# Centred rows for V and z2 of the first two blocks, their transposes by DMA, and z2's weights loaded from two queues

## The chip, the cores and the metric

The kernel runs on one core of a Trainium2 chip. The metric is the device time of one execution in microseconds (us). A core has five engines that run beside each other: TensorE (PE, matmuls into PSUM), VectorE (DVE), ScalarE (ACT), GpSimd (POOL) and SyncE (SP). SP mostly issues DMAs; ACT and POOL can issue DMAs too. Each engine executes its own instructions in order, and engines wait for each other by semaphores.

## What is computed

For x of 2048 rows and 512 columns, xn is x normalised by row. The output is x, plus a sliding attention (32 heads of 16, 8 positions 2 apart), plus a gated MLP whose gate mixes all rows:

```python
xn = _layernorm(x, axis=-1)                      # (x - m) / sqrt(v + eps)
# branch A: q, k, v = xn @ wqkv; each row attends to rows s, s-2, ..., s-14; then @ wo
# branch B:
z = _gelu(einsum('bsd,df->bsf', xn, w_in))       # 2 x 896 columns
z1 = z[..., :896]
z2 = _layernorm(z[..., 896:], axis=-1)
g = einsum('ts,bsf->btf', w_sp, z2) + b_sp[None, :, None]
branch_B = einsum('bsf,fd->bsd', z1 * g, w_out)
return x + A + branch_B
```

All tensors are bf16; sums are in f32.

## The kernel before

The rows are cut in 16 blocks of 128. `build_kernel` makes a list of tasks (matmul groups, activations, DMAs) with what they read and write, and `Plan.schedule` simulates them with estimated durations to find one fixed order for each engine and the PSUM banks. `Plan.emit` then writes each engine's instructions in that order, with the waits that the data needs. So each engine's order is fixed before the run: where a real landing is later than the planner thinks, the engine stands. The planner's inputs include priorities (`prio`), lists of names that must follow each other on an engine (line 1003 on), and a table `land` with assumed landing times of the first loads.

What happens to a block b at the start:

- `ld_x(b)` (L514) loads 128 rows of x. x0 and x1 go out from ACT's queue, the others from SP's.
- `ln_block(b)` (L592 on) computes the row statistics on DVE, `bnst` (L599), `bnag` (L601) and `vpe` (L609, variance plus eps), then 1/sqrt on POOL (`rstd`, L611), then the normalised rows on DVE (`norm`, L623).
- For blocks 0 to 3 (`b < NXT`) PE transposes the normalised rows by four matmuls with the identity (`xTr`, L579), and ACT copies them from PSUM to `xnT` (`xTe`, L587). For blocks 4 to 15 a DMA transposes them, issued by SP (`xTd`, L617).
- `v_block(b)` (L654) makes V of the block by four matmuls; ACT evicts it (`Ve`, L663), POOL writes it to a scratch in DRAM (`Vw`, L668).
- `z2_block(b)` (L766) makes 896 columns of z2 in two halves of 448, four matmuls each. The halves of the weights are two loads, w_in2a (L524) and w_in2b (L530). ACT applies the gelu (L774) and sums squares (L779).

V of blocks 0 and 1 does not wait for the normalised rows. PE transposes raw x (`xTx`, L579), ACT copies it to `xcT` (`xTc`, L606), V is made of raw rows, and the mean is taken out afterwards: four matmuls of ones with V's weights give the weights' column sums (`cs`, L638), ACT stores them negated (`cse`, L642), DVE adds mean times column sum to V in PSUM (`fix`, L660), and `Ve` scales with rstd. z2 of blocks 0 and 1 waits for the normalised and transposed rows.

Then `qk_pair` (L677) makes Q and K of four blocks at a time (it reads `xnT` of all four and the weights wq and wk, `ldq` and `ldk`, L536). DVE multiplies Q and shifted K (L698, L703); PE sums over the head dimension (`red`, L713); the softmax follows. PE makes z1 (L812) and then, for most of the time, the mixing of the rows (`g_group`, L907); the output blocks (L963, L972) end the kernel.

SP's DMAs at the start are wv (two halves, L518), x2, w_in2a, w_in2b, x3 to x7, wq, wk, x8 to x15; then the transposes of blocks 4 to 7, w_in1 (L853), and the transposes of blocks 8 to 15. Before x0 lands PE multiplies ones (`warm`, L560).

Of the kernel before, what the change touches and what calls it, by code (L numbers as in the profile page):

```python
# [9 lines left out]
F32 = mybir.dt.float32  # L10
# [328 lines left out]
def build_kernel(nc, A_x, A_wqkv, A_wo, B_x, B_w_in, B_w_sp, B_b_sp, B_w_out, out, report=False, emit=True):  # L339
# [12 lines left out]
    NWARM = 8  # L352
# [18 lines left out]
    place(3584, w_in1=0, tg=0, On=2048, xcT=0, ncs=1024)  # L371
# [14 lines left out]
    for name, n in (("prime", 4), ("mx", 128), ("Zb", 256), ("Z", 128), ("maskt", 128), ("st6", NB * 6),  # L386
                    ("mv", NB * 2), ("vpe", NB), ("rstd", NB), ("s1", NB), ("s2", NB), ("m2", NB), ("msq", NB),
                    ("vpe2", NB), ("rstd2", NB), ("mhalf", 4)):
        foff[name] = fb
        fb += n  # L390
# [5 lines left out]
    with ExitStack() as es:  # L396
# [69 lines left out]
        for hf in range(2):  # L466
            for b in range(2):
                R1(("xcT", b, hf), "xcT", 256, 512 * b + 256 * hf)
            R(("xnT", 0, hf), "sb", [(off["xnT"] + dc * S, off["xnT"] + dc * S + 128) for dc in (2 * hf, 2 * hf + 1)])
        R1("ncs", "ncs", 1024)  # L470
        R1("bbc", "bbc", S)
        R1("w_in1", "w_in1", 3584)
        R("w_in2a", "sb", [(off["w_in2"] + dc * 896, off["w_in2"] + dc * 896 + 448) for dc in range(4)])
# [27 lines left out]
        ncs = A("ncs", 1024).bitcast(F32)  # L501
# [21 lines left out]
        def ld_win2a():  # L523
            dma("sp", lambda e: e.dma_start(  # L524
                AC(off["w_in2"], [[896, 4], [1, 448]]),
                B_w_in[:, 896:1344].rearrange("(c p) n -> p c n", p=128)),
                512 * 448 * 2, "w_in2a", writes=["w_in2a"], name="ldwin2a")
# [45 lines left out]
        def pe_tr(src, keys, name):  # L573
            bk = plan.bank(name)

            def tr(t):
                last = None
                for dc in range(4):
# [3 lines left out]
            T("pe", tr, reads=keys + ["ident"], writes=[bk], est=(430.0 if name == "xTx0" else 4 * c_mm(128)), name=name)  # L582
            return bk

        def to_xnT(b, bk, halves, prio=0, after=()):
            for d0, dn in (((0, 2), (2, 2)) if halves else ((0, 4),)):
                T("act", (lambda d0, dn: lambda a: a.activation(  # L587
                    AC(off["xnT"] + d0 * S + 128 * b, [[S, dn], [1, 128]]),
                    P(bk, 128 * dn, 128 * d0).rearrange("p (c n) -> p c n", c=dn), ACTF.Copy))(d0, dn),
                  reads=[bk], writes=([("xnT", b, d0 // 2)] if halves else [("xnT", b)]), est=c_act(128 * dn),  # L590
                  name="xTe%d_%d" % (b, d0), prio=prio)

        def ln_block(b):
# [4 lines left out]

            T("dve", lambda v: v.bn_stats(Fv("st6", 6, 6 * b), xin), reads=xk, writes=[("st6", b)],  # L599
# [3 lines left out]
            if b < 2:  # L603
                bc = pe_tr(xin, xk, "xTx%d" % b)
                for hf in range(2):
                    T("act", (lambda hf: lambda a: a.activation(A("xcT", 256, 512 * b + 256 * hf), P(bc, 256, 256 * hf),  # L606
                                                                ACTF.Copy))(hf),
                      reads=[bc], writes=[("xcT", b, hf)], est=c_act(256), name="xTc%d_%d" % (b, hf), prio=-1)
            T("dve", lambda v: v.tensor_scalar(Fv("vpe", 1, b), Fv("mv", 1, 2 * b + 1), LN_EPS, None, ALU.add),  # L609
              reads=[("mv", b)], writes=[("vpe", b)], est=140, name="vpe%d" % b, prio=-1.5 + b * 0.1)  # L610
# [3 lines left out]
            if b < NXT:  # L614
                to_xnT(b, pe_tr(xn, [("xn", sl)], "xTr%d" % b), b == 0)
# [13 lines left out]
        def xTv(b, dc):  # L629
            return AC(off["xnT"] + dc * S + 128 * b, [[1, 128]])  # L630

        def colsum():
            bk = plan.bank("cs")
            for hf in range(2):
                def mm(t, hf=hf):
                    last = None
                    for dc in (2 * hf, 2 * hf + 1):
                        last = t.matmul(P(bk, 512), ones[:, 0:128], A("wv", 512, 512 * dc), start=(dc == 0),  # L638
                                        stop=(dc == 3))
                    return last  # L640
                T("pe", mm, reads=[("wv", hf)], writes=[bk], est=2 * c_mm(512) * (1 if hf else 2), name="cs_%d" % hf, prio=2)
            T("act", lambda a: a.activation(ncs, P(bk, 512), ACTF.Copy, scale=-1.0), reads=[bk],  # L642
              writes=["ncs"], est=c_act(512), name="cse", prio=-0.5)

        def v_block(b):
# [4 lines left out]
            for hf in range(2):  # L650
                def mm(t, hf=hf):
                    last = None
                    for dc in (2 * hf, 2 * hf + 1):
                        last = t.matmul(P(bk, 512), A("xcT", 128, 512 * b + 128 * dc) if b < 2 else xTv(b, dc),  # L654
                                        A("wv", 512, 512 * dc), start=(dc == 0), stop=(dc == 3))
                    return last
                T("pe", mm, reads=[("xcT", b, hf) if b < 2 else ("xnT", b), ("wv", hf)], writes=[bk],
                  est=2 * c_mm(512) * (1.5 if (b, hf) == (0, 0) else 1), name="V%d_%d" % (b, hf), prio=(2 if b < 4 else 60 + b))
            if b < 2:
# [3 lines left out]
            T("act", lambda a: a.activation(vn.rearrange("p (d h) -> p d h", d=16),  # L663
                                            PC(bk.col(), [[1, 16], [16, 32]]), ACTF.Copy,
                                            scale=Fv("rstd", 1, b) if b < 2 else 1.0),
              reads=[bk] + ([("rstd", b)] if b < 2 else []), writes=[("Vn", sl)], est=c_act(512), name="Ve%d" % b,
              prio=4)
# [91 lines left out]
        def z2_block(b):  # L759
            bk = plan.bank("z2_%d" % b, 2)  # L760
            for hf in range(2):
                for dcs in (((0, 1), (2, 3)) if b == 0 and hf == 0 else ((0, 1, 2, 3),)):
                    def mm(t, hf=hf, dcs=dcs):
                        last = None
                        for dc in dcs:
                            last = t.matmul(P(bk, 448, 512 * hf), xTv(b, dc),  # L766
                                            AC(off["w_in2"] + 896 * dc + 448 * hf, [[1, 448]]),
                                            start=(dc == 0), stop=(dc == 3))
                        return last
                    T("pe", mm, reads=([("xnT", 0, dcs[0] // 2)] if len(dcs) == 2 else [("xnT", 0, 0), ("xnT", 0, 1)] if b == 0 else [("xnT", b)]) +  # L770
                      ["w_in2b" if hf else "w_in2a"],
                      writes=[bk], est=len(dcs) * c_mm(448),
                      name="z2_%d_%d" % (b, hf) + ("b" if dcs == (2, 3) else ""), prio=12 + 4 * b)
            T("act", lambda a: a.activation(A("z2", FH, FH * b).rearrange("p (t n) -> p t n", t=2),  # L774
                                            PC(bk.col(), [[512, 2], [1, 448]]),
                                            ACTF.Gelu_apprx_tanh, accum_out=Fv("s1", 1, b)),
              reads=[bk], writes=[("z2", b), ("s1", b)], est=c_act(FH, accum=True),
# [49 lines left out]
        colsum()  # L827
        v_block(0)
        v_block(1)
        lnd += [ln_block(b) for b in range(2, NB)]  # L830
# [172 lines left out]
        for names in (["warm%d" % wi for wi in range(NWARM)] +  # L1003
                      ["xTx0", "cs_0", "V0_0", "xTx1", "cs_1", "V0_1", "xTr0", "V1_0", "xTr1", "V1_1",
                       "z2_0_0", "z2_0_0b", "z2_0_1", "xTr2", "z2_1_0", "z2_1_1", "V2_0", "V2_1", "xTr3", "z2_2_0"],
                      ("rstd4", "Vw0"),
                      ("bnst0", "bnag0", "vpe0", "bnst1", "bnag1", "vpe1", "norm0", "norm1", "bnst2", "bnag2",
                       "vpe2", "norm2", "fix0", "bnst3", "bnag3", "vpe3", "fix1", "norm3", "bnst4", "bnag4", "vpe4",
                       "bnst5"),
                      ["bnst%d" % b for b in range(5, NB)],  # L1010
                      ("xTc0_0", "xTc0_1", "xTc1_0", "xTc1_1", "xTe0_0", "xTe0_2", "cse", "xTe1_0", "xTe2_0", "z2g0",
                       "Ve0", "xTe3_0", "z2g1", "Ve1", "Ve2", "z2s0"), ("V10_1", "Q3_3")):
# [57 lines left out]
```

## Time and profile before

| | |
|---|---|
| time, median of 3 runs | 237.40 us (236.48, 237.40, 237.75) |
| profiled execution: time | 237.29 us |
| profiled execution: span of the trace | 236.1 us, 2974 instructions |
| what lies around the span | 1.2 us |
| DVE busy | 207.4 us (88%) |
| ACT busy | 96.5 us (41%) |
| L907 (mixing of rows), PE | 96.6 us |
| L677 (Q, K), PE | 28.7 us |
| L766 (z2), PE | 26.0 us |
| L654 (V), PE | 15.6 us |
| granted TensorE clock, mean | 1.0 |

How to read it: an engine's busy time is the time in which one of its compute instructions runs; issuing DMAs and waiting are not in it. Matmuls are pipelined, so the duration of one (0.379 us for 512 columns) is longer than the distance between two starts. Times in the timelines count from the start of the span. "idle before <-X" is the time in which the engine stood, and what it waited for last. "To landing" of a DMA is from its issue to the arrival of its last part.

### The profile page before, as it was taken

What the parts mean: (1) busy time and instruction counts of PE and PEld (TensorE: products, weight loads), DVE (VectorE), ACT (ScalarE), POOL (GpSimd) and SP (SyncE); (2) the same over time, 40 slices, a digit from 0 to 9 for tenths busy, and PEclk for the clock granted to TensorE, in tenths of its full rate; (3) what the DMA queues carried; (4) which work ended last, traced back from release to release, by engine and by line L of the source; (5) the groups of instructions that cost most, each with busy time, mean ns of one, the idle gap of its engine ahead of it and who ended that gap; (6) DMA issues with size and microseconds to landing.
All of it is one profiled execution on the core that took longest, in us unless ns stands there. A gap on an engine that the chain in (4) does not pass through costs nothing.

```text
span 236.1 us, 2974 instructions
## 1 busy us (share of the span) xinstructions
PE 231.7 (98%) x1114; PEld 109.1 (46%) x1135; DVE 207.4 (88%) x269; ACT 96.5 (41%) x145; POOL 32.7 (14%) x56
## 2 busy tenths in 40 slices
PE   8999999999999999999999999999999999999996
PEld 3455555555444444444444444444444444444443
DVE  3799899999998899999699998986989997999432
ACT  3598889888967895510120531111111111000000
POOL 2259650311733100000000000000000000000000
PEclk9999999999999999999999999999999999999999
DMA  7998969991048325430999999998995959936432
GB/s 211 352 283 163 243 146 217 195 202 44 22 165 260 92 85 69 104 118 0 226 347 252 225 266 180 200 304 187 346 258 175 261 161 303 193 95 181 135 96 69
DMA packets 82013, 43.86 MB, mean 186 GB/s; under 512 B 54336, under 2 KB 81360, under 8 KB 82000
## 3 DMA queue, kind: packets, MB, share of 16 engines
q1 hardware_dynamic: 80768, 41.27, 71.5%
q0 software_dynamic: 800, 2.11, 2.8%
q10 hardware_dynamic: 432, 0.30, 0.6%
q8 instruction: 9, 0.15, 0.3%
q14 instruction: 4, 0.03, 0.1%
HBM read 26.35 MB, written 4.21 MB: 129 GB/s over the span
## 4 chain that ended last, share of the span: by engine, by line
PE 94%; DMA 3%; SPq 1%; ACT 1%; issue 1%; DVE 0%
PE ps L907 41%; PE ps L677 12%; PE ps L972 10%; PE ps L812 10%; PE ps L766 9%; PE ps L963 6%; PE ps L654 5%; DMA arena<-in_B_w_in_dram 3%; PE ps L713 1%; ACT arena L774 0%; SPq L518 0%; ACT arena L587 0%; PE ps L579 0%; SPq L514 0%; SPq L524 0%
## 5 line engine op out<-in xcount | busy, mean ns | idle before, releaser
L907 PE MATMUL ps<-arena 128*128 128x512 bf16 x439 | 96.6, 379 | 0.5
L907 PEld LDWEIGHTS ps<-arena 128*128 128x128 bf16 x448 | 43.7, 98 | 53.1 <-issue 0.4
L915 ACT ACTIVATE arena<-ps 128x1024 bf16<-128x1024 f32 (+1 forms) x16 | 14.7, 917 | 78.0 <-PE ps L907 78.0
L698 DVE TENSOR_TENSOR arena<-arena 128x4096 bf16<-128x4096 bf16 x16 | 36.5, 2282 | 0.1
L935 DVE TENSOR_TENSOR arena<-arena 128x4096 bf16<-128x4096 bf16 x16 | 36.4, 2283 | 0.0
L938 DVE TENSOR_TENSOR arena<-arena 128x2048 bf16<-128x2048 bf16 (+1 forms) x32 | 29.9, 948 | 0.0
L677 PE MATMUL ps<-arena 128*128 128x512 bf16 x126 | 28.7, 379 | 0.1
L703 DVE TENSOR_TENSOR arena<-arena 128x4096 bf16<-128x4096 bf16 x12 | 27.4, 2287 | 0.1
L972 PE MATMUL ps<-arena 128*128 128x512 bf16 (+2 forms) x117 | 26.9, 366 | 0.1
L766 PE MATMUL ps<-arena 128*128 128x448 bf16 x128 | 26.0, 352 | 0.5 <-DMA arena<-in_B_w_in_dram 0.5
L812 PE MATMUL ps<-arena 128*128 128x512 bf16 x110 | 24.4, 379 | 0.1
L978 DVE TENSOR_TENSOR arena<-ps,arena 128x512 bf16<-128x512 f32 (+2 forms) x17 | 11.2, 658 | 11.7 <-PE ps L972 11.7
L677 PEld LDWEIGHTS ps<-arena 128*128 128x128 bf16 x128 | 14.5, 113 | 13.0
L766 PEld LDWEIGHTS ps<-arena 128*128 128x128 bf16 x128 | 12.3, 98 | 12.7 <-ACT arena L642 0.7
L686 ACT ACTIVATE arena<-ps 128x1024 bf16<-128x1024 f32 x16 | 16.3, 1021 | 4.4 <-PE ps L677 4.1
L972 PEld LDWEIGHTS ps<-arena 128*128 128x128 bf16 x119 | 11.4, 98 | 12.8
L812 PEld LDWEIGHTS ps<-arena 128*128 128x128 bf16 x112 | 10.9, 98 | 13.2 <-ACT arena L818 0.3
L963 PE MATMUL ps<-arena 128*128 128x512 bf16 (+2 forms) x66 | 16.5, 366 | 0.1
L774 ACT ACTIVATE arena<-ps 128x896 bf16<-128x896 f32 x16 | 14.6, 914 | 3.2 <-PE ps L766 3.1
L818 ACT ACTIVATE arena<-ps 128x1024 bf16<-128x1024 f32 (+1 forms) x16 | 13.9, 923 | 4.9 <-PE ps L812 4.8
L654 PE MATMUL ps<-arena 128*128 128x512 bf16 x60 | 15.6, 379 | 0.2
L779 ACT ACTIVATE arena<-arena 128x896 bf16<-128x896 bf16 x16 | 15.1, 945 | 0.0
(61 smaller groups left out, 168.5 us busy)
## 6 DMA issues: line engine op xcount, KB each, us to landing
arena<-vscr SPq DMA_DIRECT2D x16, 1024.0 KB, 7.1
arena<-in_A_x_dram SPq DMA_DIRECT2D x30, 128.0 KB, 3.6
vscr<-arena POOLq DMA_DIRECT2D x16, 128.0 KB, 3.0
out_dram<-arena SPq DMA_DIRECT2D x15, 128.0 KB, 1.8
arena<-in_A_wqkv_dram SPq DMA_DIRECT2D x2, 512.0 KB, 6.9
arena<-in_B_w_in_dram SPq DMA_DIRECT2D x2, 448.0 KB, 6.1
arena<-in_B_w_in_dram SPq DMA_DIRECT2D x1, 896.0 KB, 5.9
arena<-in_B_w_out_dram SPq DMA_DIRECT2D x1, 896.0 KB, 4.9
```

The lines of the kernel that those rows point to most:

```text
L654: last = t.matmul(P(bk, 512), A("xcT", 128, 512 * b + 128 * dc) if b < 2 else xTv(b, dc), A("wv", 512, 512 * dc), start=(dc == 0), stop=(d ...
L677: last = t.matmul(P(bk, 512, 512 * which), AC(off["wqk"] + 2048 * which + 512 * dc + c, [[4, 128]]), AC(off["xnT"] + dc * S + 512 * j, [[1 ...
L686: T("act", lambda a: a.activation(AC(qo, [[ko - qo, 2], [1, 512]]), P(bk, 1024).rearrange("p (t n) -> p t n", t=2), ACTF.Copy, scale=0.5), ...
L698: T("dve", (lambda pbv, qb, kb: lambda v: v.tensor_tensor(pbv, qb, kb, ALU.mult))(pbv, qb, kb), reads=rd, writes=[("pb", s_)], est=c_tt(40 ...
L703: T("dve", (lambda av, bv: lambda v: v.tensor_tensor(av, av, bv, ALU.add))(av, bv), reads=[("pb", 1)], writes=[("pb", acc)], est=c_tt(4096 ...
L766: last = t.matmul(P(bk, 448, 512 * hf), xTv(b, dc), AC(off["w_in2"] + 896 * dc + 448 * hf, [[1, 448]]), start=(dc == 0), stop=(dc == 3))
L812: last = t.matmul(P(bk, 512, 512 * i), AC(off["w_in1"] + 896 * dc + 128 * fc, [[1, 128]]), AC(off["xnT"] + dc * S + 512 * j, [[1, 512]]), ...
L907: last = t.matmul(P(bk, 512, 512 * i), AC(off["z2"] + FH * sh + 128 * fc, [[1, 128]]), AC(off["wT%d" % r_] + sh * 512, [[1, 512]]), start= ...
L935: T("dve", lambda v: v.tensor_tensor(tv, tv, av, ALU.mult), reads=[("attn", b)], writes=[("Vs", sv)], est=c_tt(4096), name="pv%d" % b, pri ...
L938: T("dve", (lambda n: lambda v: v.tensor_tensor(A("Vs", n, 4096 * sv), A("Vs", n, 4096 * sv), A("Vs", n, 4096 * sv + n), ALU.add))(n), wri ...
L963: last = t.matmul(P(bk, cn), AC(off["OT"] + 512 * tb + 128 * cc, [[1, 128]]), AC(off["wo"] + 512 * cc + c0, [[1, cn]]), start=(cc == 0), s ...
L972: last = t.matmul(P(bk, cn), AC(off["z1T"] + fc * S + 128 * tb, [[1, 128]]), AC(off["w_out"] + 512 * fc + c0, [[1, cn]]), start=False, sto ...
```

## The change

V and z2 of blocks 0 and 1 are now both made of centred rows. DVE sums each row of raw x (`sum`), then computes 512 x - sum (`cen`). PE transposes that in two halves, in banks of their own, and ACT copies each half with the factor 1/512 to `xcT`. V and z2 of the two blocks read `xcT`, and rstd is applied behind PSUM, as the scale of the V eviction and of the gelu. The column sums and the fixes are gone. The normalised rows of blocks 0 and 1 are still made, for Q, K and z1; they are now transposed by DMA (`xTd0`, `xTd1`) like those of blocks 4 to 15, so `xTr` and `xTe` remain for blocks 2 and 3 only.

w_in2a is cut in two loads: the first 256 rows go out from ACT's queue behind x1, the other 256 from SP's behind wv. x3 goes ahead of w_in2b. The warm-up has 15 matmuls and not 8, three of them placed between the transposes of block 0 and V.

The orders written out by hand change with it: on DVE norm0 and norm1 stand behind vpe3; on SP wk and then x8 to x15 stand behind the two new transposes; on PE z2_1_0 stands ahead of z2_0_1, and all of z2_3 ahead of Q0. From block 12 on, vpe is computed for two blocks at once. The planner's constants change: tolerance 30 and not 50, DMA rate 270 and not 300, DMA latency 1300 and not 1600, overlap 0 and not 40, and other assumed landings.

```diff
-    NWARM = 8
+    NWARM = 15
...
-        def ld_win2a():
-            dma("sp", lambda e: e.dma_start(
-                AC(off["w_in2"], [[896, 4], [1, 448]]),
-                B_w_in[:, 896:1344].rearrange("(c p) n -> p c n", p=128)),
-                512 * 448 * 2, "w_in2a", writes=["w_in2a"], name="ldwin2a")
+        def ld_win2a(kh, eng):
+            dma(eng, lambda e: e.dma_start(
+                AC(off["w_in2"] + 1792 * kh, [[896, 2], [1, 448]]),
+                B_w_in[256 * kh:256 * kh + 256, 896:1344].rearrange("(c p) n -> p c n", p=128)),
+                256 * 448 * 2, ("w_in2a", kh), writes=[("w_in2a", kh)], name="ldwin2a%d" % kh)
...
         ld_x(1, "act")
+        ld_win2a(0, "act")
         ld_wv(0)
         ld_wv(1)
+        ld_win2a(1, "sp")
         ld_x(2, "sp")
-        ld_win2a()
+        ld_x(3, "sp")
         ld_win2b()
-        ld_x(3, "sp")
         ld_x(4, "sp")
...
-            n_ = 512 if wi < 6 else 128
+            n_ = 512 if wi < 8 else 128
...
+            if b < 2:
+                xc = A("xc", 512, 512 * b)
+                T("dve", lambda v: v.tensor_reduce(Fv("sx", 1, b), xin, AX.X, ALU.add), reads=xk, writes=[("sx", b)],
+                  est=685, name="sum%d" % b, prio=-2)
+                T("dve", lambda v: v.tensor_scalar(xc, xin, 512.0, Fv("sx", 1, b), ALU.mult, ALU.subtract),
+                  reads=xk + [("sx", b)], writes=[("xc", b)], est=c_ts(512), name="cen%d" % b, prio=-2)
+                for hf in range(2):
+                    bc = plan.bank("xTc%d_%d" % (b, hf))
+                    pe_tr(xc, [("xc", b)], "xTc%d_%d" % (b, hf), bc, (2 * hf, 2 * hf + 1))
+                    T("act", (lambda hf, bc: lambda a: a.activation(A("xcT", 256, 512 * b + 256 * hf),
+                                                                    P(bc, 256, 256 * hf), ACTF.Copy,
+                                                                    scale=1.0 / 512))(hf, bc),
+                      reads=[bc], writes=[("xcT", b, hf)], est=c_act(256), name="xcT%d_%d" % (b, hf), prio=-1)
...
-            if b < NXT:
-                to_xnT(b, pe_tr(xn, [("xn", sl)], "xTr%d" % b), b == 0)
+            if 2 <= b < NXT:
+                bk = plan.bank("xTr%d" % b)
+                pe_tr(xn, [("xn", sl)], "xTr%d" % b, bk, range(4))
...
         def xTv(b, dc):
+            if b < 2:
+                return A("xcT", 128, 512 * b + 128 * dc)
             return AC(off["xnT"] + dc * S + 128 * b, [[1, 128]])
+        def xsc(b):
+            return Fv("rstd", 1, b) if b < 2 else 1.0
-        def colsum():
...
-            if b < 2:
-                T("dve", lambda v: v.scalar_tensor_tensor(P(bk, 512), ncs, Fv("mv", 1, 2 * b), P(bk, 512),
-                                                          ALU.mult, ALU.add),
-                  reads=["ncs", ("mv", b)], writes=[bk], est=690, name="fix%d" % b, prio=1)
...
-                                            ACTF.Gelu_apprx_tanh, accum_out=Fv("s1", 1, b)),
+                                            ACTF.Gelu_apprx_tanh, scale=xsc(b), accum_out=Fv("s1", 1, b)),
...
+        for names in (["warm%d" % wi for wi in range(NWARM - 3)] + ["xTc0_0", "xTc0_1"] +
+                      ["warm%d" % wi for wi in range(NWARM - 3, NWARM)] +
+                      ["V0_0", "xTc1_0", "xTc1_1", "V0_1", "V1_0", "V1_1", "z2_0_0", "z2_1_0", "z2_0_1", "xTr2",
+                       "z2_1_1", "V2_0", "V2_1", "xTr3", "z2_2_0", "z2_2_1", "V3_0", "V3_1", "z2_3_0", "z2_3_1", "Q0_0"],
+                      ("rstd2", "rstd1", "rstd3", "rstd4", "Vw0"), ["ldq", "xTd0", "xTd1", "ldk"] + ["ldx%d" % b for b in range(8, NB)],
+                      ("sum0", "cen0", "sum1", "cen1", "bnst0", "bnag0", "vpe0", "bnst2", "bnag2", "vpe2", "bnst1",
+                       "bnag1", "vpe1", "norm2", "bnst3", "bnag3", "vpe3", "norm0", "norm1", "norm3", "bnst4"),
+                      ["bnst%d" % b for b in range(4, NB)],
+                      ("xcT0_0", "xcT0_1", "xcT1_0", "xcT1_1", "Ve0", "xTe2", "Ve1", "z2g0", "xTe3", "z2g1", "Ve2", "z2g2",
+                       "z2s0"), ("V10_1", "Q3_3"), ("z2_3_1", "Q0_1"), ("z2_3_1", "Q0_2"), ("z2_3_1", "Q0_3")):
...
-        plan.schedule(tol=50.0, dma_bw=300.0, dma_lat=1600.0, overlap=40.0,
+        plan.schedule(tol=30.0, dma_bw=270.0, dma_lat=1300.0, overlap=0.0,
```

More of the change, by code (lines that the diff above doesn't have):

```diff
@@ L370, in build_kernel @@
     place(4 * S, xnT=0, OT=0)
-    place(3584, w_in1=0, tg=0, On=2048, xcT=0, ncs=1024)
+    place(3584, w_in1=0, tg=0, On=2048, xcT=0, xc=1024)
     place(3584, w_in2=0, w_out=0)
@@ L500, in build_kernel @@
         mhalf = Fv("mhalf", 4)
-        ncs = A("ncs", 1024).bitcast(F32)
         T("pool", lambda g: g.memset(ident, 0.0), writes=["ident"], est=200, name="ident0")
@@ L581, in tr @@
                 return last
[L582 to L591, printed above, removed]
+            T("pe", tr, reads=keys + ["ident"], writes=[bk], est=len(dcs) * (107.0 if name[:4] == "xTc0" else c_mm(128)),
+              name=name)
         def ln_block(b):
@@ L629, in xTv, with xrk, xkey @@
         def xTv(b, dc):
+            if b < 2:
+                return A("xcT", 128, 512 * b + 128 * dc)
             return AC(off["xnT"] + dc * S + 128 * b, [[1, 128]])
-        def colsum():
[L633 to L643, printed above, removed]
+        def xsc(b):
+            return Fv("rstd", 1, b) if b < 2 else 1.0
+        def xrk(b):
+            return [("rstd", b)] if b < 2 else []
+        def xkey(b, hfs=(0, 1)):
+            return [("xcT", b, hf) for hf in hfs] if b < 2 else [("xnT", b)]
         def v_block(b):
@@ L1002, in build_kernel @@
         byname = {t.name: t for t in plan.tasks}
[L1003 to L1012, printed above, removed]
+        for names in (["warm%d" % wi for wi in range(NWARM - 3)] + ["xTc0_0", "xTc0_1"] +
[8 more added lines that the diff above has]
+                       "z2s0"), ("V10_1", "Q3_3"), ("z2_3_1", "Q0_1"), ("z2_3_1", "Q0_2"), ("z2_3_1", "Q0_3")):
             for n0, n1 in zip(names, names[1:]):
```

84 lines of the change are left out of this document (44 added, 40 removed).

## The prediction, written before the result was known

> **What bounds the kernel now.** The page first: TensorE (PE) is busy over nearly the whole span.
>
> ```profile
> PE 231.7 (98%) x1114; PEld 109.1 (46%) x1135; DVE 207.4 (88%) x269; ACT 96.5 (41%) x145; POOL 32.7 (14%) x56
> ```
>
> A busy PE is not yet a limit, so next the chain that ended last, for the first 12 us, then PE's timeline there. (Start, length, what.)
>
> ```profile
> 2.32 0.43 SPq L524
> 2.79 6.50 DMA arena<-in_B_w_in_dram
> ...
> 9.34 0.93 PE ps L766 x4
> 10.27 0.24 PE ps L579 x4
> ```
>
> ```profile
> 3.73 0.61 PE L579 MATMUL ps<-arena 128*128 128x128 bf16 x4
> 4.26 0.85 PE L638 MATMUL ps<-arena,const-bfloat16-1.0 128*128 128x512 bf16 x2
> 4.95 0.60 PE L654 MATMUL ps<-arena 128*128 128x512 bf16 x2
> 5.38 0.39 PE L579 MATMUL ps<-arena 128*128 128x128 bf16 x4
> ...
> 7.34 0.59 PE L654 MATMUL ps<-arena 128*128 128x512 bf16 x2
> 8.22 0.92 PE L766 MATMUL ps<-arena 128*128 128x448 bf16 x4 [0.28 <-DMA arena<-in_B_w_in_dram]
> 9.34 0.93 PE L766 MATMUL ps<-arena 128*128 128x448 bf16 x4 [0.21 <-DMA arena<-in_B_w_in_dram]
> ```
>
> Until 9.34 us PE follows loads (the second half of z2's weights lands at 9.30); after it the chain is PE nearly without a gap to 234.2. So this change is worth what it does to the moment at which PE's unbroken stream begins, less every gap that it opens behind it. Pitches from the rows: two 512-column matmuls in 0.60, one lasting 0.379, so 0.216 each; 448 columns 0.189; 128 columns 0.056. A block of z2 is 8 x 0.189 = 1.51, V of a block 0.86.
>
> The loads run at the full rate of the DMA engines (start:end, ..., DMA share, GB/s):
>
> ```profile
> 5.50:6.50 1.00, 1.00 (x10) 0.53 (x8) 0.60 (x3) 0.66 (x2) 0.63 (x2) 1.00 1.12 336
> ...
> 7.50:8.50 1.00, 0.72 (x5) 0.22 (x3) 0.44 (x3) 1.00 (x3) 0.41 (x1) 1.00 1.08 373
> 8.50:9.50 1.00, 0.79 (x5) 0.21 (x4) 0.82 (x2) 0.03 (x1) 0.14 (x1) 1.00 1.09 370
> ```
>
> So order and bytes set landings, and 128 KB cost 0.35 us.
>
> **The change, part by part.**
>
> *Work removed.* Four column-sum matmuls (4 x 0.216 = 0.86) and eight transposes of xn0 and xn1 (8 x 0.056 = 0.45) leave PE: 1.31, all ahead of 9.34. ACT loses cse (0.60), xTe0 (0.66) and xTe1 (0.62); DVE loses two fixes (0.75 each). ACT and DVE have idle time there, so these count only through the order below.
>
> *Later first matmul.* PE now transposes raw x0 at 3.73. It will wait for a sum and a centring on DVE. The sum, a reduction of 512 elements, isn't in the trace: half of the 1024-element reduction (L728, 1.217) is 0.61, all of it 1.217, and statistics over the same 512 bf16 take 0.683 (L599). I take 0.685. Centring is a norm, 0.41 (L623). sum0 3.71 to 4.40, cen0 4.43 to 4.84, first transpose 4.96 (0.115 from DVE's end to PE, as after norm1). ACT copies from 5.27 to 5.65 (0.38, L606), the next 0.28 later; first V matmul at 5.83 (0.18 from ACT's end to PE, as after cse) where it is 4.95 now. Then xTc1 at 6.26, V0_1 6.49, xcT1_0 6.58 to 6.96, V1_0 7.14 (a gap of 0.2), V1_1 7.57, end 8.00. So 1.31 less of PE work buys nothing here: V ends at 8.00, where it ends at 7.77 now.
>
> *Seven more warm-up matmuls.* Two of 512 columns and five of 128, by L560's cold pitches of 0.427 and 0.107, are 1.39; twelve end at 4.70, before cen0 does, three fall in the wait for ACT's copy. Free; without that cover 0.3.
>
> *z2's first weights on two queues.* w_in2a goes ahead of x2, so 128 KB less lie before it. Now x2 lands at 5.7 (issue 1.81, 3.9 to landing), w_in2a at 8.1 (2.32, 5.8). 448 KB at 0.36 MB/us would need 1.24, to 6.95, so this execution held its last part 1.15 longer. It comes at 7.75, or at 6.6 undisturbed. Either is before 8.00: z2_0_0 runs 8.00 to 8.76, z2_1_0 follows at once (it needs only w_in2a; new here) to 9.51. ACT's queue issues one DMA more (0.45) ahead of its table load; its first copy is due at 5.27 and the load would end near 3.5, so that is hidden; uncovered 0.45.
>
> The Trainium skill ("DMA: Bandwidth & Descriptors", section "Issuing engines are not separate DMA queues") says that DMAs started from several engines share the same 16 DMA engines, and that a second issuer saves only issue time. That speaks against the two queues. The rows of 336 to 373 GB/s agree, and by the rule the gain of w_in2a is its place ahead of x2 alone; since z2_0_0 waits for V until 8.00 either way, the sum is the same with or without it.
>
> *w_in2b.* x3 now goes ahead of it: 128 KB more, 9.30 + 0.35 = 9.65, first matmul 9.70; undisturbed 8.5, and PE comes at 9.51. z2_0_1 to 10.45, xTr2 to 10.67 (norm2 ends at 9.46), z2_1_1 to 11.43. V2 needs ACT's copy of xTr2 (10.88 to 11.47), so 11.65: a gap of 0.22, since only 4 and not 8 matmuls cover it. V2 12.51, xTr3 12.73, z2_2 14.25, V3 15.11, z2_3 16.62, then Q0_0. Now Q0_0 starts at 15.31 with z2_3 still to do, that is 16.82. The stream is **0.2 ahead**, and 0.4 if w_in2a and w_in2b are not held up; I take 0.3. The gelus of z2_0 and z2_1 take a scale by pointer, 0.09 more each (the two V evictions with one take 0.685, those without 0.597); ACT has that room.
>
> *Transposes by DMA.* norm0 and norm1 are put behind vpe3 on DVE: sum1, cen1, four statistics with their aggregates, and norm2 lie ahead. By 0.69 + 0.18 + 0.15 a block, norm0 ends at 10.8 and norm1 at 11.1 (6.13 and 7.00 now). SP then issues two transposes at 1.2 to 1.3 each:
>
> ```profile
> L617 SPq DMA_TRANSPOSE arena<-arena x4: 1222/1295/1647, 14.5 to 18.8; - x4
> ...
> DMA to landing us min/median/max: 3.0/4.4/4.9
> ```
>
> xTd0 10.9, xTd1 12.1 to 13.35; landing at 15.1 with 3.0. Q0_0, the first to read all four blocks, is due at 16.62: hidden, by 1.5.
>
> *What stands behind them on SP.* K's weights (ldk), issued at 6.8 now, wait for xTd0 and xTd1 and go out at 13.35. 512 KB: w_out's 896 KB took 4.9 from issue, less 384 KB (1.04) is 3.9, the low end, landing at 17.25; w_in1's 896 KB, issued right behind a transpose as ldk will be, took 5.9, so 4.9, landing at 18.25. K0_0 is due at 16.62 + 0.86 = 17.48. The wait is 0 to 0.85; the row nearest is w_in1's, so I take **0.8 lost**. x8 to x15 (issued 7.8 to 12.1 now) follow from 13.8 to 17.6 and land at 18.6 to 21. Block 8's statistics, at 16.4 now, come 2.2 late on DVE. PE's first reader of that stream at risk is L713 at 64.64; DVE's last add before it ends at 63.19, and four waits of 0.16 to 0.52 between 19.9 and 29.4 (1.1 in all) give slack: 2.2 - 1.1 - 0.5 (PE's own shift) is under the 1.45 there. Cost 0; without those waits 0.3. xTd4 to xTd7, now at 14.5 to 20.1, follow x15; behind its landing at 21 the last lands at 24.4 to 25.8, and Q1, now at 25.4, is due at 25.2 + 0.8 = 26.0. Covered; if not, 0.5.
>
> **Sum.** The profiled execution took 237.29 (span 236.1, 1.2 around it), 0.1 under the median of 237.40. 237.29 - 0.3 + 0.8 = **237.8**.
>
> **Rivals.**
>
> *No wait for K's weights.* If ldk takes w_out's 3.9, it lands at 17.25 and nothing is late: 237.29 - 0.3 = **237.0**. For it: w_in1 had four transposes ahead of it, ldk two.
>
> *The work saved shows in full.* If DVE's sum and ACT's copies are shorter, V could end near 7.2 and z2_0_0 start there; the stream is then 1.3 ahead: **236.0**. It needs w_in2b by 8.8 as well. Against it: the chain sum, centre, transpose, copy, matmul has four hops, each with a row.
>
> *Slower: SP's queue stretches.* A transpose issued behind loads that are still running (14.5, behind x8 to x15) took 4.9 to land, the next 4.5. xTd0 goes out at 10.9 behind x4 to x7 and ldq, which lands at 12.7. With 4.5 xTd1 lands at 16.6, 1.5 later, and ldk behind it at 19.75: K0_0 waits 2.3, **239.3**. It decides as soon as xTd1 lands after 15.9 (K0_0's wait then passes 1.6). For it: two of the four early transposes took 4.5 and more. Against: the queue ahead drains at 12.7, two microseconds after xTd0's issue, and the same queue's later transposes took down to 2.4.
>
> *The clock.* Before 4.95 the pitch of 512 columns is 0.40 (L638: two in 0.85), after it 0.216. If the gap that PE has at 4.70 puts that step off, V0 and V1 (eight matmuls) lose up to 8 x 0.19 = 1.5: **239.3** with the K wait. The Trainium skill ("TensorE: Matmul & The Clock Gate", Part 1) has the gate open after about 3.4 us of sustained activity, in a free-running window; by that a gap of 0.3 closes nothing, but the window's phase can shift the step.
>
> **Chances.** Forecast (K0_0 waits 0.3 to 1.3) 0.43; no wait 0.24; in full 0.11; stretched queue 0.19; clock 0.03. The forecast's upper edge touches 238.5, so a part of it counts as slower. More or less than 0.5% (1.2 us) is about what a measurement of this kernel can tell from no change: faster 0.11, same 0.60, slower 0.29. The range for 8 in 10 leaves out most of the full saving and half of the stretched queue: 236.3 to 239.3.
>
> **What would show it.** First L654 matmul near 5.8; z2_1_0 directly behind z2_0_0 near 8.0; Q0 (L677) at 16.4 to 16.7; a gap of PE behind Q0's first four matmuls ended by in_A_wqkv (forecast 0.8, none for 237.0, over 1.6 for the slow rival, there with L617's landing over 4); later no gap on PE but the small issue ones. A gap at L713, or at Q1 (near 26) ended by L617, would prove me wrong on what I called covered; so would z2_0_0 before 7.5.

## The result, and the profile after

| | before | after |
|---|---|---|
| time, median of 8 runs each | 237.09 us (236.48 to 237.75) | 238.23 us (237.94 to 238.81) |
| ratio, 95% interval | | 1.0052 (1.0038 to 1.0065) |
| profiled execution, time and span | 237.29, 236.1 us | 238.30, 237.1 us |

The kernel is 0.5% slower, by 1.14 us between the medians and by 1.0 between the two profiled executions. The forecast was 237.8, a rise of 0.5 over the profiled 237.29 and so half of that; the time lies in its range.

The page's line of busy times, to be held against the one of before: PE works 0.2 us less, on five matmul records fewer, and the span is 1.0 longer. DVE has 8.4 us more by this line; its two sums and two centrings took 2.07, and the two fixes that are gone took 1.49. No run shows where the rest comes from, and it does not show in the account of PE's waits below.

```profile
PE 231.5 (98%) x1109; PEld 108.5 (46%) x1130; DVE 215.8 (91%) x269; ACT 95.2 (40%) x141; POOL 32.1 (14%) x56
```

Lines have moved: V is now L666, z2 L770, Q and K L682, PE's transposes L578, the DMA transposes L631. PE's timeline before, from Q0 on (start, length, what, and the idle time before it with its releaser):

```profile
15.31 7.07 PE L677 MATMUL ps<-arena 128*128 128x512 bf16 x31
22.22 3.19 PE L766 MATMUL ps<-arena 128*128 128x448 bf16 x16
25.24 7.07 PE L677 MATMUL ps<-arena 128*128 128x512 bf16 x32
```

And after the change:

```profile
5.56 0.59 PE L666 MATMUL ps<-arena 128*128 128x512 bf16 x2 [0.28 <-ACT arena L599]
5.99 0.39 PE L578 MATMUL ps<-arena 128*128 128x128 bf16 x4
6.21 1.57 PE L666 MATMUL ps<-arena 128*128 128x512 bf16 x6
7.62 2.43 PE L770 MATMUL ps<-arena 128*128 128x448 bf16 x12
9.94 0.40 PE L578 MATMUL ps<-arena 128*128 128x128 bf16 x4
10.18 0.92 PE L770 MATMUL ps<-arena 128*128 128x448 bf16 x4
11.26 0.81 PE L666 MATMUL ps<-arena 128*128 128x512 bf16 x3 [0.16 <-issue]
...
16.25 1.03 PE L682 MATMUL ps<-arena 128*128 128x512 bf16 x4
18.45 6.24 PE L682 MATMUL ps<-arena 128*128 128x512 bf16 x27 [1.18 <-DMA arena<-in_A_wqkv_dram]
24.52 1.68 PE L770 MATMUL ps<-arena 128*128 128x448 bf16 x8
26.22 1.46 PE L682 MATMUL ps<-arena 128*128 128x512 bf16 x6
```

V starts at 5.56 (4.95 before), but then V and three halves of z2 run through without the waits for weights that stood at 8.22 and 9.34. Q0's first four matmuls start at 16.25 with z2_3 done. Before, they started at 15.31 with z2_3 (1.51) still to do, so the stream is 0.57 ahead. Then the line that matters: behind these four (0.86 of work, to 17.11) PE stands for K's weights until 18.45. That is 1.34; the bracket counts 1.18 of it, since the last matmul's tail is not idle. A last small gap of 0.18 follows at Q1: the eight z2 matmuls from 24.52 end at 26.04, and block 7's transpose (xTd7) lands at 26.09. From there to the end the two streams keep their distance: Q1 starts at 25.24 before and 26.22 after, 0.98 later, and the first mixing matmul (L907 before, L910 now) at 98.23 and 99.20, 0.97 later. The account is -0.57 + 1.34 + 0.18 = **+0.95**, within 0.1 of the whole difference.

Why the weights are late is in the chain of waits over that stretch, read upwards from `18.45`:

```profile
2.33 5.11 DMA arena<-in_A_x_dram
7.44 0.02 issue
7.46 0.70 DVE fpool L603
...
11.65 0.41 DVE arena L637
12.07 0.61 DVE fpool L603
...
13.69 0.14 SPq L631
13.83 0.04 issue
13.88 4.53 DMA arena<-in_A_wqkv_dram
18.41 0.05 issue
18.45 4.08 PE ps L682 x18
```

K's load goes out at 13.88, directly when SP is done with L631. The chain puts DVE's work up to 13.69 ahead of that, but SP was not waiting then: its own timeline has it issuing L631 from 11.24 on.

```profile
6.21 0.43 SPq L536 DMA_DIRECT2D arena<-in_A_wqkv_dram  x1
11.24 2.59 SPq L631 DMA_TRANSPOSE arena<-arena  x2
13.88 0.58 SPq L536 DMA_DIRECT2D arena<-in_A_wqkv_dram  x1
14.50 4.02 SPq L514 DMA_DIRECT2D arena<-in_A_x_dram  x8
18.56 5.91 SPq L631 DMA_TRANSPOSE arena<-arena  x4
```

From 6.64 to 11.24 SP issues nothing: it stands at the first new transpose, whose input norm0 DVE writes only at 11.2, behind two sums, two centrings and four statistics. DVE also stands 0.89 in that stretch, until 7.46, for x2, which lands at 7.44 (5.68 before) because w_in2a now goes ahead of it. The transposes then take 2.59 to issue. What is behind them goes out late: K's weights by 7.1 (6.80 before, 13.88 now), x8 to x15 by 6.3 to 6.7, the transposes of blocks 4 to 7 by some 4 (14.49 to 18.83 before, 18.56 to 23.20 now). The landings are 4 to 6 later: K's weights at 18.41 (14.22 before), x15 at 23.08 (17.04), xTd7 at 26.09 (21.81).

### The profile page after: what moved, and what is told of

Same layout as the page of the kernel before. It is cut to its first block, busy times and chain, and to the rows that moved or that the text cites. A ratio compares the mean times of both kernels' runs of the same rounds, so it can differ in the third digit from the quotient of the medians.

```text
span 237.1 us, 2958 instructions
## 1 busy us (share of the span) xinstructions
PE 231.5 (98%) x1109; PEld 108.5 (46%) x1130; DVE 215.8 (91%) x269; ACT 95.2 (40%) x141; POOL 32.1 (14%) x56
## 4 chain that ended last, share of the span: by engine, by line
PE 90%; DMA 4%; DVE 3%; issue 1%; SPq 1%; ACT 0%; POOL 0%; DVEq 0%
PE ps L910 41%; PE ps L682 11%; PE ps L813 10%; PE ps L975 10%; PE ps L770 8%; PE ps L966 6%; PE ps L666 4%; DMA arena<-in_A_x_dram 2%; DMA arena<-in_A_wqkv_dram 2%; DVE fpool L603 1%; ACT arena L775 0%; PE ps L718 0%; SPq L518 0%; DVE arena L981 0%; DVE fpool L605 0%
## 5 line engine op out<-in xcount | busy, mean ns | idle before, releaser
L910 PE MATMUL ps<-arena 128*128 128x512 bf16 x439 | 96.6, 379 | 0.5
L910 PEld LDWEIGHTS ps<-arena 128*128 128x128 bf16 x448 | 43.7, 98 | 53.1 <-issue 0.4
L941 DVE TENSOR_TENSOR arena<-arena 128x2048 bf16<-128x2048 bf16 (+1 forms) x32 | 30.6, 958 | 1.0
L682 PE MATMUL ps<-arena 128*128 128x512 bf16 x126 | 28.9, 379 | 1.3 <-DMA arena<-in_A_wqkv_dram 1.2
L770 PE MATMUL ps<-arena 128*128 128x448 bf16 x128 | 26.0, 352 | 0.0
L813 PE MATMUL ps<-arena 128*128 128x512 bf16 x110 | 24.4, 379 | 0.1
L682 PEld LDWEIGHTS ps<-arena 128*128 128x128 bf16 x128 | 14.3, 113 | 14.7 <-DMA arena<-in_A_wqkv_dram 1.7
L770 PEld LDWEIGHTS ps<-arena 128*128 128x128 bf16 x128 | 12.4, 98 | 11.7 <-DMA arena<-in_B_w_in_dram 0.2
L813 PEld LDWEIGHTS ps<-arena 128*128 128x128 bf16 x112 | 10.9, 98 | 13.3 <-ACT arena L819 0.3
L666 PE MATMUL ps<-arena 128*128 128x512 bf16 x60 | 15.2, 379 | 0.7 <-ACT arena L599 0.3
L775 ACT ACTIVATE arena<-ps 128x896 bf16<-128x896 f32 x14 | 12.8, 915 | 3.3 <-PE ps L770 3.3
L981 DVE TENSOR_TENSOR arena<-ps,arena 128x512 bf16<-128x512 f32 (+2 forms) x17 | 10.4, 653 | 3.3 <-PE ps L975 2.8
```

The source lines that it names most:

```text
L666: last = t.matmul(P(bk, 512), xTv(b, dc), A("wv", 512, 512 * dc), start=(dc == 0), stop=(dc == 3))
L682: last = t.matmul(P(bk, 512, 512 * which), AC(off["wqk"] + 2048 * which + 512 * dc + c, [[4, 128]]), AC(off["xnT"] + dc * S + 512 * j, [[1 ...
L770: last = t.matmul(P(bk, 448, 512 * hf), xTv(b, dc), AC(off["w_in2"] + 896 * dc + 448 * hf, [[1, 448]]), start=(dc == 0), stop=(dc == 3))
L813: last = t.matmul(P(bk, 512, 512 * i), AC(off["w_in1"] + 896 * dc + 128 * fc, [[1, 128]]), AC(off["xnT"] + dc * S + 512 * j, [[1, 512]]), ...
L910: last = t.matmul(P(bk, 512, 512 * i), AC(off["z2"] + FH * sh + 128 * fc, [[1, 128]]), AC(off["wT%d" % r_] + sh * 512, [[1, 512]]), start= ...
L941: T("dve", (lambda n: lambda v: v.tensor_tensor(A("Vs", n, 4096 * sv), A("Vs", n, 4096 * sv), A("Vs", n, 4096 * sv + n), ALU.add))(n), wri ...
```

## The experiments

Theory A: the loss is this in-order queue of SP, and it is paid where K0 waits. Rivals: B, that the transposes by DMA are themselves too slow for Q0; C, that the late x8 to x15 hold DVE up; D, that the new order of z2's weights on two queues costs time; E, that a late K load would have been hidden in the kernel before too. The diffs are against the kernel after unless another is named; of long lines they show only the part that changes. Ratios are to the kernel before on the same chip: 237.10 (23 runs) for wk_first, pe_tr01, one_queue and before_late_wk; on another chip 236.72 (29 runs) for wk_x89_first, old_loads, before_new_loads and warm8, and 236.89 (15 runs) for q_first, wk_x89_look and old_loads_z25. So across these groups ratios are compared, not times. The planner runs anew for every edit, so an edit to one list can also move work on another engine.

### wk_first: K's weights ahead of the two transposes

```diff
-["ldq", "xTd0", "xTd1", "ldk"]
+["ldq", "ldk", "xTd0", "xTd1"]
```

> The changed kernel with one edit: SP issues K's weights ahead of the two new transposes, as before the change; all else as changed. If SP's order alone makes the loss, the weights land near 13.3 (Q's at 11.9 plus 512 KB at 0.36 MB/us), the gap of 1.34 between Q0 and K0 closes, and the time falls from 238.2 to about 236.9, 0.1% under the kernel before. If the transposes by DMA are slow as such, they now land behind the weights: xTd1 after 17.4, Q0 itself waits 1.2 and the time stays at 238.2. In between: xTd1 near 16.5 and a wait of 0.3 at Q0, 237.2.

Measured: 237.10 us (12 runs), ratio 1.0011 (0.9998 to 1.0023). By the ratios (1.0052 and 1.0011) one swap in a list gives 1.0 us back. PE's timeline:

```profile
16.52 7.07 PE L682 MATMUL ps<-arena 128*128 128x512 bf16 x32
23.43 2.43 PE L770 MATMUL ps<-arena 128*128 128x448 bf16 x12
```

All 32 matmuls of Q0 and K0 run as one piece. K's weights land at 13.63. The transposes are still there and are as long: they land at 14.65 and 15.24, before Q0 needs them at 16.52, so B falls. x8 lands at 16.49 and x9 to x15 at 19.34 to 22.00, 1.9 to 5.0 later than before, so C as the main cause falls too. A gap of 0.19 stays at Q1, and Q0 is 0.3 ahead: together 0.1, as the profiled execution (237.22 against 237.29) has it. Not all of the gain is the load's own: the planner has also put twelve z2 matmuls ahead of Q1, where the kernel after has eight. Behind eight, by these rows, Q1 would have been due at 24.94, 0.86 before xTd7 landed (25.80). pe_tr01, next, keeps eight.

### pe_tr01: PE transposes the normalised rows of blocks 0 and 1

```diff
-            if 2 <= b < NXT:
+            if b < NXT:
...
-"z2_2_0", "z2_2_1", "V3_0"
+"z2_2_0", "z2_2_1", "xTr0", "xTr1", "V3_0"
...
-["ldq", "xTd0", "xTd1", "ldk"]
+["ldq", "ldk"]
...
-"z2g1", "Ve2", "z2g2"
+"z2g1", "Ve2", "xTe0", "xTe1", "z2g2"
```

> The changed kernel, but the normalised rows of blocks 0 and 1 are transposed by PE and copied by ACT again (behind z2 of block 2), so that SP has no transpose ahead of K's weights and of x8 to x15. If SP's order makes the loss: no gap at K0 and none at Q1 (1.34 and 0.18 gone), 0.45 of PE work back, 237.1 to 237.2, the kernel before within 0.1. If centred rows or the weights' order cost something by themselves, it stays at 238.2 or rises to 238.7.

Measured: 237.33 us (12 runs), 1.0009 (0.9998 to 1.0021). PE pays 0.45 for eight transposes (Q0 at 17.02), and neither K0 nor Q1 has a gap. PE's order at Q1 is that of the kernel after, so it is the queue without the two transposes, and not the planner, that closes both gaps. The two DMA transposes save PE 0.45 and cost it, in this queue, about three times that (1.34 + 0.18).

### one_queue: both halves of z2's first weights from SP

```diff
-        ld_win2a(0, "act")
         ld_wv(0)
         ld_wv(1)
+        ld_win2a(0, "sp")
         ld_win2a(1, "sp")
```

> The changed kernel with both halves of w_in2a issued by SP, behind wv and ahead of x2; nothing of them on ACT's queue. If the DMA engines are the limit and the second queue saves only issue time: w_in2a lands within 0.3 of 7.2, z2_0_0 starts at 7.6 as now, 238.2. If the second queue moves data sooner: w_in2a lands 0.4 or more later, z2_0_0 starts at 8.0 or later, and the time rises by what is lost there, 0.2 to 0.5.

Measured: 237.99 us (4 runs), 1.0047 (1.0031 to 1.0063), the time of the kernel after. The halves land at 5.96 and 6.69, where in the kernel after, with two queues, they land at 7.00 and 7.22. That difference need not be the queue's: in q_first, with two queues too, they land at 6.22 and 6.56. The second queue brings nothing that shows in the time; it is not the cause of the loss either, so that part of D falls. The rule of the Trainium skill cited in the prediction ("DMA: Bandwidth & Descriptors", section "Issuing engines are not separate DMA queues") fits this: with one issuer the time is the same.

### before_late_wk: the kernel before, with K's weights behind x15

```diff
-"Ve0", "xTe3_0", "z2g1", "Ve1", "Ve2", "z2s0"), ("V10_1", "Q3_3")):
+"Ve0", "xTe3_0", "z2g1", "Ve1", "Ve2", "z2s0"), ("V10_1", "Q3_3"), ("ldx15", "ldk")):
```

> The kernel before with one edit: SP issues K's weights behind x15. If a late load of them is paid in full: they land near 17.0, K0 (due at 16.2) waits 0.9, and the time is 0.8 to 1.0 over the kernel before, 238.0. If slack behind takes it up: K0 waits, but the time stays within 0.3 of the kernel before.

Measured: 238.04 us (4 runs), 1.0045 (1.0030 to 1.0060). Nothing of the change is in this kernel, only the late load, and it is slower by nearly as much. PE's timeline:

```profile
15.12 1.03 PE L677 MATMUL ps<-arena 128*128 128x512 bf16 x4
16.87 3.43 PE L677 MATMUL ps<-arena 128*128 128x512 bf16 x15 [0.72 <-DMA arena<-in_A_wqkv_dram]
```

The weights land at 16.82. The four Q0 matmuls end at 15.98, so PE stands for 0.89, and the medians differ by 0.94. A late K load is paid in full, even with z2_3 still to be done: E falls, because PE's order is fixed and z2_3 stands behind K0.

### wk_x89_first and wk_x89_look: K's weights, x8 and x9 ahead of the transposes

```diff
-["ldq", "xTd0", "xTd1", "ldk"] + ["ldx%d" % b for b in range(8, NB)]
+["ldq", "ldk", "ldx8", "ldx9", "xTd0", "xTd1"] + ["ldx%d" % b for b in range(10, NB)]
```

> The changed kernel with K's weights, x8 and x9 issued ahead of the two new transposes, in SP's idle time after Q's weights. If SP's order is what is left to win, the transposes of blocks 4 to 7 go out some 0.9 sooner, the gap of 0.19 ahead of Q1 closes and the time is about 236.9, level with or just under the kernel before. If two more loads ahead of xTd0 and xTd1 put these past 16.3, Q0 waits up to 0.5 and it is 237.3 to 237.6.

Measured: 237.77 us (12 runs), 1.0034 (1.0023 to 1.0046): slower than wk_first (1.0011), against what was expected. Its profiled execution, 237.31, was among its fastest and shows no gap at Q0, K0 or Q1. A second profiled execution of the same kernel is wk_x89_look:

> The kernel with K's weights, x8 and x9 first once more, for a second profile: its first profiled execution was the shortest of its runs (237.09), the others lay at 237.3 to 238.1. If Q0 waits for its transposes in those, this profile shows a gap of 0.3 to 0.6 there with L631 landing past 16.1; if it shows no gap before 30 us, the difference lies elsewhere.

It took 237.96, span 236.5 against 235.8. Its timeline has a gap that the first lacked, at Q1 and not at Q0, where it was expected:

```profile
25.19 3.19 PE L682 MATMUL ps<-arena 128*128 128x512 bf16 x14 [0.43 <-DMA arena<-arena]
```

Q1 stands 0.59 for xTd7, which lands at 24.95; in the first execution it lands at 23.98. Of the 0.7 between the spans this is 0.59. The landing of a transpose moved by one microsecond between two executions of one program, so a wait that "is covered" by less than that is not covered in every run. This gap is not the whole reason why the kernel is slower than wk_first: in both executions 0.37 of PE's lead is lost between Q1 and the mixing (24.55 to 97.91 and 25.19 to 98.55, where the kernel before takes 25.24 to 98.23; 0.20 of it is a wait for ACT at L813), and the time outside the span is 1.47 and 1.46 us, where the other profiled executions have 1.23 to 1.27. No run shows why.

### q_first: after's own load order, all of Q0 ahead of K0

```diff
-("z2_3_1", "Q0_3")):
+("z2_3_1", "Q0_3"), ("Q0_3", "K0_0")):
```

> The changed kernel with SP's order as changed (K's weights late), but PE makes all four Q groups of the first four blocks ahead of the first K group. If the late weights cost only because K0 stands next in PE's order, the gap of 1.34 closes though the weights land at 18.4 as now: Q0 to Q3 take PE from 16.3 to 19.7, and the time falls to 237.0. If PSUM banks stand against it (Q3 needs the pair that z2 of block 3 holds until ACT is done, about 17.5), 0.3 to 0.6 of the gap stay, now ended by ACT: 237.4.

Measured: 238.47 us (4 runs), 1.0073 (1.0047 to 1.0099). The wait for K's weights is gone, and the kernel is no faster, where 237.0 was expected:

```profile
16.42 7.07 PE L682 MATMUL ps<-arena 128*128 128x512 bf16 x32
23.83 1.67 PE L770 MATMUL ps<-arena 128*128 128x448 bf16 x8 [0.34 <-DMA arena<-arena]
26.07 2.11 PE L682 MATMUL ps<-arena 128*128 128x512 bf16 x9 [0.57 <-DMA arena<-arena]
```

With 12 Q0 matmuls more ahead of K0, the weights come in time. But z2_4 then stands 0.50 for xTd4 (landed 23.69) and Q1 0.73 for xTd7 (25.73): 1.23 in place of 1.34 + 0.18. In the kernel after, K0's wait covers them. So the cause is not the one load but the queue: what stands behind the two transposes lands later than before (here K's weights by 3.8, xTd4 by 4.3, xTd7 by 3.9), and whichever of it PE reaches first is what PE waits for. In wk_first the load's move also brings the rest forward: xTd4 lands at 22.67 there, 23.62 in the kernel after.

### old_loads and before_new_loads: what the new load order is worth

old_loads is wk_first with the old order (z2's first weights on SP behind x2, still as two loads, x3 behind w_in2b); before_new_loads is the kernel before with the new order.

```diff
-        ld_win2a(0, "act")
         ld_wv(0)
         ld_wv(1)
-        ld_win2a(1, "sp")
         ld_x(2, "sp")
-        ld_x(3, "sp")
+        ld_win2a(0, "sp")
+        ld_win2a(1, "sp")
         ld_win2b()
+        ld_x(3, "sp")
```

> The changed kernel with K's weights first, and with the old order of the first loads: w_in2a whole behind x2 on SP, x3 behind w_in2b. If that order is part of what brought PE's stream forward: w_in2a lands near 8.0, z2_0_0 starts 0.4 later than now (7.6) and the time rises by 0.3 to 0.4, to 237.5. If V's end sets z2_0_0, it starts within 0.1 of now and the time stays at 237.1.

> The kernel before with the new order of the first loads alone (w_in2a in two halves on two queues ahead of x2, x3 ahead of w_in2b). z2_0_0 waits for ACT's copy of the column sums there (8.0), so w_in2a's earlier landing buys nothing, and w_in2b comes up to 0.35 later: 237.1 to 237.4. If the loads alone are what the change gains, z2_0_0 starts before 8.0 and the time falls by 0.3, to 236.8.

Measured: old_loads 236.69 us (10 runs), 0.9999 (0.9988 to 1.0010); before_new_loads 236.81 us (10 runs), 0.9999 (0.9988 to 1.0010). In old_loads w_in2a lands at 7.01 and z2_0_0 starts at 7.89, directly behind V, as it does in wk_first (7.79). The kernel before gains nothing from the new order, within 0.3 us; for the changed kernel old_loads (0.9999) is level with wk_first (1.0011) or a little faster, and the intervals overlap. So the order gains nothing that shows where K's weights go out early.

What this leaves of D: no run has the old order with K's weights late. In the kernel after, the chain of K0's wait begins with x2's landing, and DVE stands 0.89 for it; in old_loads x2 lands at 5.63, DVE does not stand, and norm0 starts at 10.00 (10.81 in the kernel after). So the new order can have had up to 0.9 us of part in K0's wait of 1.34, as an estimate from these rows. It is not tested.

### warm8: wk_first with the old number of warm-up matmuls

```diff
-    NWARM = 15
+    NWARM = 8
...
-            n_ = 512 if wi < 8 else 128
+            n_ = 512 if wi < 5 else 128
```

> The changed kernel with K's weights first, and with 8 warm-up matmuls and not 15 (five of 512 columns, three of 128 behind the first transposes), so that PE idles from 3.0 to 4.7. If the step of the pitch from 0.43 to 0.216 hangs on PE's activity before it, V0 and V1 run at 0.40 or more for a while: V ends up to 1.5 later and the time is 237.5 to 238.6. If the step comes by itself near 4.9, V's pitch is 0.216 from the first, and the time stays at 237.1.

Measured: 238.04 us (4 runs), 1.0054 (1.0034 to 1.0075); wk_first has 1.0011 (0.9998 to 1.0023), so by the ratios 1.0 us more.

```profile
4.75 0.59 PE L578 MATMUL ps<-arena 128*128 128x128 bf16 x4 [1.62 <-DVE arena L594]
...
5.60 1.04 PE L666 MATMUL ps<-arena 128*128 128x512 bf16 x2
...
6.86 2.16 PE L666 MATMUL ps<-arena 128*128 128x512 bf16 x6
8.85 2.43 PE L770 MATMUL ps<-arena 128*128 128x448 bf16 x12
```

Two V matmuls take 1.04 where they take 0.59 in the kernel after: a pitch of 0.43 in place of 0.216, until 8.3. (In the kernel before eight were enough: PE went straight on with raw x0.) V ends at 8.85 (7.79 in wk_first). In this execution, the fastest of the four, waits that wk_first has behind V take up over half of that; Q1 is 0.47 late. So the seven additional warm-ups do earn their place: the change puts a DVE step ahead of PE's first real matmul, and without them PE idles 1.62 there.

### old_loads_z25: old_loads, with all of z2_5 ahead of Q1

```diff
-("z2_3_1", "Q0_3")):
+("z2_3_1", "Q0_3")) + tuple(("z2_5_1", "%s1_%d" % (q, c)) for q in "QK" for c in range(4)):
```

> The changed kernel with K's weights first and the old order of the first loads, and with all of z2 of block 5 ahead of Q1 on PE. The gap of 0.46 there, which waits for the transpose of block 7, closes, and with PE's stream 0.3 to 0.5 ahead the time is 236.2 to 236.4, 0.15 to 0.2% under the kernel before. If DVE, which gets the products of blocks 4 to 7 some 0.7 later, passes that on to PE at the sum over heads, the gap turns up there and the time stays level with the kernel before.

Measured: 236.69 us (11 runs), 0.9995 (0.9986 to 1.0005), where 236.2 to 236.4 was expected.

```profile
16.17 7.07 PE L682 MATMUL ps<-arena 128*128 128x512 bf16 x32
23.08 3.19 PE L770 MATMUL ps<-arena 128*128 128x448 bf16 x16
26.11 2.10 PE L682 MATMUL ps<-arena 128*128 128x512 bf16 x9
```

No gap is left at K0 or Q1, and yet the median is that of old_loads. By the profiles it is 0.6 ahead of the kernel before (236.68 against 237.29), but that execution of before lies on the long side of its runs (before_late_wk, the same kernel up to there, starts Q0 at 15.12 and not 15.31), and by the medians the two are level. With no gap of PE left to the late loads, the 1.31 us of PE work that the change removes gives less than can be measured (at most 0.3 us by the interval).

## Why the prediction was right, and where its sizes were off

The result has the forecast's sign and mechanism (the stream a little ahead, then more lost than gained where K0 waits for its weights), and +1.0 in place of +0.5. By its steps:

- **Later first matmul.** Sum 0.683 (0.685 taken), centring 0.353 (0.41), V at 5.56 (5.83), V's end at 7.62 (8.00). x0 landed 0.2 earlier than in the profile of before (3.48 and 3.69), and that is most of the difference. The claim that 1.31 less of PE work buys nothing here held: V ended at 7.77 before.
- **z2's weights.** w_in2a was taken at 7.75, or 6.6 undisturbed, and came at 7.22; w_in2b at 9.65, or 8.5, and came at 8.99. The prediction took the lateness of w_in2a before (8.09) for a thing of one execution; before_late_wk, which has the same single load, has it at 7.88, while old_loads and old_loads_z25, with two halves in the same place, have the second at 7.01 and 6.99. So the cut into halves may be the reason; no run tests it alone. z2_1_0 follows z2_0_0 directly, as said. V2's gap is 0.32 (0.22).
- **The stream ahead**, 0.3 taken, 0.4 as the upper end: 0.57 in this execution, between 0.30 (wk_first) and 0.73 (one_queue) in the other kernels with this change and 15 warm-ups whose PE does not transpose blocks 0 and 1. In this execution V's earlier end is what it was short of.
- **K0's wait**, the term of the sum that was most off: 0.8 taken, 1.34 measured. Its landing came out nearly right (18.25, was 18.41), in part by luck: the issue was 0.53 later (13.35, was 13.88) and the way to landing 0.37 shorter (4.9, was 4.53). The later issue has a term that the prediction left out: w_in2a ahead of x2 also makes x2 late, and DVE's 0.89 of standing for it lies ahead of norm0. What moved more was the other end: K0 was due at 17.11 and not 17.48, since the stream was further ahead. A stream that arrives earlier at a fixed landing only waits longer, so the two terms were not independent: every tenth gained ahead of K0 is lost at K0. The sum was really K0's start, 18.45 against 18.25, and that was 0.20 off. The prediction's own figures also do not agree with each other here: it gained 0.3 ahead of K0, but priced the wait from a K0 due at 17.48, which has the stream 0.2 ahead. Of the 0.45 by which the account exceeds the forecast, 0.20 is K0's start, 0.18 the gap at Q1 and 0.07 that sum. The wait of 1.34 also lies just above the 0.3 to 1.3 that the prediction gave to its own case, and Q0 at 16.25 just ahead of its 16.4 to 16.7.
- **Q1 "covered".** It stood 0.18 for xTd7 (landing 26.09, forecast at most 25.8), the sign that the prediction had named against itself. It had x15 landing at 21, and x15 landed at 23.08; and its "now at 25.4" for Q1 is where the chain counts from, while the timeline has Q1's start at 25.24. q_first shows that the cover was K0's wait: without it the same late queue costs 0.50 and 0.73 at z2_4 and Q1.
- **x8 2.2 late on DVE**, cost 0: x8 landed at 18.72, DVE stood 1.53 for it, and no gap of PE shows at the reduction (L718). The cost was right, the reason was not: the planner had put the reduction 6.8 later in PE's time, at 71.45 (64.64 before). DVE's last add before it ends at 68.86, 5.7 later than the 63.19 before, so with the reduction in its old place and this order on DVE, PE would have stood.
- **The rivals.** "No wait" (237.0) is wk_first's time, reached by an edit and not by a quicker load. "The work saved shows in full" (236.0) needed V's end near 7.2; it was at 7.62. "Stretched queue" (239.3) needed 4.5 to landing for xTd1; it took 2.4. The step of the pitch was not put off: V runs at 0.216 from 5.56 on. It can come later in another execution: q_first's first two V matmuls take 0.80 and not 0.59. warm8 shows what the idle stretch costs without the added warm-ups: 1.06 at V's end, where up to 1.5 was forecast. It keeps three warm-ups between the transposes and V, so these alone do not cover it.

What stays open: the two medians differ by 1.14, the profiles by 1.0 and the account gives 0.95; the runs do not say where the last tenth or two lies. The stream's lead varies from 0.30 (wk_first) to 0.64 (wk_x89_look) with the landings of the first loads (x2 at 7.71 and 7.36, w_in2b at 9.31 and 8.95); why these vary is not settled either.

## What to carry to other kernels

An operation that is moved to an in-order DMA queue is priced by what stands behind it: here 2.6 us of issue and a 4.6 us wait for a late input made every later load go out 6 to 7 us late and land 4 to 6 us late. Put the instruction whose input comes latest behind the loads that need no input, and look for the first reader of each load behind it. A gain ahead of a fixed landing is not a gain; it makes the wait longer, and removing one such wait (q_first) only shows the next.

## What the runs showed of the hardware

**K's load starts slowly.** By the windows of the kernel after (start:end, busy shares, granted clock, DMA share, GB/s), K's load is issued at 13.88, behind two transposes (landing 14.12 and 14.96) and ahead of x8 to x15:

```profile
14.00:15.00 1.00, 1.00 (x7) 0.47 (x5) 0.96 (x4) 1.00 (x4) 0.75 (x2) 1.00 0.60 159
15.00:16.00 1.00, 1.00 (x7) 0.51 (x6) 0.88 (x5) 1.00 (x3) 0.75 (x3) 1.00 0.76 186
16.00:17.00 1.00, 1.00 (x7) 0.45 (x4) 0.91 (x3) 0.57 (x2) 1.00 (x2) 1.00 0.97 304
17.00:18.00 1.00, 0.28 (x2) 0.00 (x0) 0.18 (x2) 1.00 (x3) 0.75 (x3) 1.00 1.05 373
```

While the second transpose is still landing the rate is 159; in the microsecond after its landing it is 186, then 304, and only from 17 on 373, the rate of the loads in the kernel before. At the last rate throughout, 512 KB would take 1.4 us; from issue it took 4.53. That the transposes ahead are the reason is not shown: at the start of the kernel before, with nothing ahead, loads issued from 0.80 on move nothing until 1.50, 31 and 80 GB/s in the next two half microseconds, 266 from 2.50 and 381 from 3.00.

**The step of PE's pitch comes later behind an idle stretch, and its moment moves.** The pitch of 512 columns falls from 0.43 to 0.216 at a moment that the starts of PE's matmuls show; the granted clock in the profile's windows reads 1.00 on both sides of it. In the twelve profiled executions without a long idle stretch the step lies between 3.9 (before_late_wk, wk_x89_first) and 6.3 (q_first), that is 3.0 to 5.4 after PE's first matmul at 0.84. In warm8, with eight warm-ups and 1.62 of idle, it lies at 8.27, later than in any of them, and 3.5 after PE resumed at 4.75. The Trainium skill ("TensorE: Matmul & The Clock Gate", Part 1) has the gate open after about 3.4 us of sustained activity, which fits the distance in warm8; the spread of 2.4 here is much wider than the half microsecond either way that the page gives, and the measurement decides.
